# Transposes of P once per kv-head in half-height pairs, with Q/K loads apart from V loads, in a grouped-query attention kernel

## Chip, cores, metric

One core of one Trainium2 chip. The metric is the device time of one execution in microseconds (us), median of several runs.

## The reference

```python
B, Hq, Hkv, Sq, Sk, D = 8, 16, 8, 256, 512, 256      # q, k, v in bf16
k = jnp.repeat(k, 2, axis=1)                          # two query heads share one kv-head
v = jnp.repeat(v, 2, axis=1)
scores = jnp.einsum("bhqd,bhkd->bhqk", q, k) * D ** -0.5
p = softmax(scores, axis=-1)
return jnp.einsum("bhqk,bhkd->bhqd", p, v)
```

There are 64 pairs of batch and kv-head ("heads" below). Each has 2 × 256 query rows, so four tiles of 128 rows ("steps"): 256 steps in all.

## The kernel before

Per step, TensorE makes scores S (2 matmuls, 512 columns), transposes the 128x512 tile of P (4 transposes of 128x128) and multiplies by V (4 matmuls, 257 columns; the 257th gives the row sums). VectorE finds the row minimum of the negated scores and copies the transposed P out of PSUM; ScalarE takes the exponential and copies the output out; GpSimd normalises. The tensor queue is software-pipelined: transposes run 2 steps and P·V 4 steps behind the scores.

```python
    LAG_PT = 2; LAG_PV = 4; LAG_OC = 4; LAG_RC = 5
    NSB = 3; NPTB = 2; NOB = 3; NP = 3; NPT = 4; NO = 20      # buffers
    # ... PSUM: S 3 banks, PT 2 banks, O 3 banks
        @block.vector
            for t in range(NSTEP + LAG_RC):
                # ... minimum of step t (L217), then
                u = t - LAG_PT
                    dve.wait_ge(sem_PT, u + 1)
                    dve.tensor_copy(                                   # L227
                        PT_sb[:, u % NPT, :, :],
                        PT_ps[:, u % NPTB, 0:NC * P].rearrange("p (c q) -> p c q", c=NC),
                    ).then_inc(sem_PTe, 1)
        @block.tensor
            for t in range(NSTEP + LAG_PV):
                # ... scores of step t, two matmuls (L268)
                w = t - LAG_PT
                if 0 <= w < NSTEP:
                    pe.wait_ge(sem_P, w + 1)
                    if w >= NPTB:
                        pe.wait_ge(sem_PTe, w - NPTB + 1)
                    for c in range(NC):
                        mm = pe.transpose(                             # L281
                            PT_ps[:, w % NPTB, c * P:(c + 1) * P],
                            P_sb[:, w % NP, c * P:(c + 1) * P],
                            ident[:],
                        )
                    mm.then_inc(sem_PT, 1)
                # ... P.V of step t - LAG_PV, four matmuls (L300)
        @block.sync
            for pi, (b, h0, h1) in enumerate(pieces):
                # ... waits; load Q and K of the piece with DMA transposes, then its V
```

## Time and profile before

| | before |
|---|---|
| time | 293.57 us (293.41 to 293.71, 13 runs) |
| span of the profile | 291.7 us |
| PE / DVE / ACT busy | 98% / 93% / 85% |
| one head (4 steps), from scores to the next head's scores | 4.38 us |

"Busy" counts an engine as busy while any record of it is open. TensorE's records overlap (a transpose's is 219 ns long, and the next one starts 56 ns after it), so its costs are read from the distances between starts. The prediction shows the lines and how they are read.

### The profile page before, as it was taken

Reading aid. Unit: us, or ns where it says so; the run is one execution under the profiler, and the core shown is the slowest. Engines: PE = TensorE matmul, PEld = TensorE weight load, DVE = VectorE, ACT = ScalarE, POOL = GpSimd, SP = SyncE. Lnnn points to the kernel's source line nnn. Section 1 sums busy time; section 2 is a strip of 40 time slices with the busy share of each in tenths; the row PEclk is TensorE's granted clock in tenths of the full one; section 3 lists DMA queues with packets and bytes.
Section 4 is the critical chain, followed back from the end, with each engine's and each line's share of the span. In section 5 each row is a group of like instructions: output and inputs, shape, how many; then the busy total and the mean of one; then the engine's idle time right before and its main releaser. Section 6 shows DMA issues by size and latency. Waiting matters only on the chain.

```text
span 291.7 us, 8061 instructions
## 1 busy us (share of the span) xinstructions
PE 284.9 (98%) x2570; PEld 215.3 (74%) x2570; DVE 270.9 (93%) x839; ACT 248.3 (85%) x514; POOL 116.9 (40%) x259
## 2 busy tenths in 40 slices
PE   7999999999999999999999999999999999999994
PEld 2677777777777777777777777777777777777772
DVE  1999999999999999999999999999999999999995
ACT  2888888888888888888888888888888888888883
POOL 1053353353353353353453453453453453453452
PEclk9999999999999999999999999999999999999999
DMA  6999999999999999999999999999999999941103
GB/s 157 231 212 247 186 264 226 256 219 253 210 337 234 183 277 221 357 236 218 253 347 243 218 234 272 327 236 219 245 359 213 215 225 276 399 174 72 74 36 112
DMA packets 154953, 67.64 MB, mean 232 GB/s; under 512 B 133792, under 2 KB 140192, under 8 KB 154912
## 3 DMA queue, kind: packets, MB, share of 16 engines
q1 hardware_dynamic: 154912, 67.12, 100.2%
q8 instruction: 22, 0.36, 0.5%
q14 instruction: 19, 0.16, 0.2%
HBM read 16.78 MB, written 16.78 MB: 115 GB/s over the span
## 4 chain that ended last, share of the span: by engine, by line
PE 95%; DMA 1%; DVE 1%; ACT 0%; SPq 0%; issue 0%; ACTq 0%
PE O_ps L300 38%; PE S_ps L268 38%; PE PT_ps L281 20%; DMA KT<-in_k_dram 1%; DVE out_sb L241 1%; ACT P_sb L207 0%; SPq L138 0%; DVE junk L217 0%; DVE rc L239 0%; DVE PT_sb L227 0%; ACT O_sb L193 0%; ACTq L192 0%
## 5 line engine op out<-in xcount | busy, mean ns | idle before, releaser
L217 DVE TENSOR_SCALAR_CACHE_REDUCE junk<-S_ps 128x512 bf16<-128x512 f32 x256 | 177.0, 692 | 17.3 <-PE S_ps L268 6.2
L182 POOL TENSOR_SCALAR out_sb<-O_sb,rc 128x256 bf16<-128x256 f32 x252 | 116.0, 479 | 170.4 <-DVE rc L247 170.4
L207 ACT ACTIVATE P_sb<-S_ps,bias 128x512 bf16<-128x512 f32 x256 | 177.4, 693 | 5.0 <-DVE junk L217 5.0
L300 PE MATMUL O_ps<-Vn,PT_sb 128*128 128x257 bf16 x1024 | 154.1, 273 | 0.0
L268 PE MATMUL S_ps<-KT,QT 128*128 128x512 bf16 x512 | 151.9, 379 | 1.2 <-DMA KT<-in_k_dram 1.0
L193 ACT COPY O_sb<-O_ps 128x257 f32<-128x257 f32 x256 | 95.5, 373 | 34.1 <-PE O_ps L300 1.0
L281 PEld LDWEIGHTS PT_ps<-ident,P_sb 128*128 128x128 bf16 x1024 | 78.3, 98 | 57.9 <-ACT P_sb L207 2.2
L227 DVE COPY PT_sb<-PT_ps 128x512 bf16<-128x512 bf16 x256 | 107.4, 420 | 0.6 <-PE PT_ps L281 0.6
L281 PE MATMUL PT_ps<-ident,P_sb 128*128 128x128 bf16 x1024 | 99.0, 219 | 0.9 <-ACT P_sb L207 0.9
L300 PEld LDWEIGHTS O_ps<-Vn,PT_sb 128*128 128x128 bf16 x1024 | 89.6, 98 | 6.3
L268 PEld LDWEIGHTS S_ps<-KT,QT 128*128 128x128 bf16 x512 | 56.9, 113 | 5.3 <-issue 1.8
L217 DVE DVE_READ_ACCUMULATOR junk<-S_ps 128x1 f32 x256 | 21.3, 83 | 0.0
L247 DVE RECIPROCAL rc<-O_sb 128x4 f32<-128x4 f32 x63 | 10.6, 168 | 0.0
L253 PE MATMUL O_ps<-const-bfloat16-1.0 128*128 128x512 bf16 x10 | 3.8, 548 | 0.8 <-PEq L320 0.8
L253 PEld LDWEIGHTS O_ps<-const-bfloat16-1.0 128*128 128x128 bf16 x10 | 1.2, 132 | 2.8 <-issue 2.7
L198 ACT ACT_TABLE_LOAD x1 | 1.3, 1283 | 0.8 <-PEq L320 0.8
L241 DVE TENSOR_SCALAR out_sb<-O_sb,rc 128x256 bf16<-128x256 f32 x4 | 1.6, 400 | 0.1
L239 DVE RECIPROCAL rc<-O_sb 128x1 f32<-128x1 f32 x4 | 0.6, 149 | 0.0
L170 POOL MEMSET Vn<- 128x64 bf16 x1 | 0.4, 380 | 0.0
L166 POOL TENSOR_SCALAR_AFFINE_SELECT ident<-const-bfloat16-1.0 128x128 bf16<-128x128 bf16 x1 | 0.3, 292 | 0.0
L320 POOL MEMSET const-float32-0.0<- 128x1 f32 x1 | 0.1, 98 | 0.3 <-issue 0.3
L165 POOL MEMSET warm<- 128x2 f32 x1 | 0.1, 99 | 0.3 <-POOLq L320 0.3
(4 smaller groups left out, 0.5 us busy)
## 6 DMA issues: line engine op xcount, KB each, us to landing
out_dram<-out_sb SPq DMA_DIRECT2D x63, 256.0 KB, 4.5
Vn<-in_v_dram SPq DMA_DIRECT2D x4, 512.0 KB, 4.5
Vn<-in_v_dram SPq DMA_DIRECT2D x4, 256.0 KB, 3.2
QT<-in_q_dram SPq DMA_TRANSPOSE x21, 9.4
KT<-in_k_dram SPq DMA_TRANSPOSE x21, 6.3
Vn<-in_v_dram SPq DMA_DIRECT2D x13, 0.5 KB, 6.2
out_dram<-out_sb SPq DMA_DIRECT2D x1, 192.0 KB, 2.5
out_dram<-out_sb SPq DMA_DIRECT2D x1, 64.0 KB, 2.2
```

Of the source, the lines that this page charges most:

```text
L182: last = g.tensor_scalar(out_sb[:, o_sl, j, :], O_sb[:, os_sl, j, 0:D], rc_t[:, os_sl, j:j + 1], 1.0, op0=ALU.mult, op1=ALU.mult,)
L193: act.copy(O_sb[:, it % NOS, j, :], O_ps[:, u % NOB, 0:D + 1]).then_inc(sem_Oc, 1)
L198: act.activation(warm[:, 1:2], warm[:, 0:1], ACTF.Exp)
L207: act.activation(P_sb[:, t % NP, :], S_ps[:, t % NSB, 0:Sk], ACTF.Exp, bias=bias_t[:, t % NBS:t % NBS + 1], scale=scale,).then_inc(sem_P, 1)
L217: dve.tensor_scalar(junk[:, t % 4, :], S_ps[:, t % NSB, 0:Sk], -scale, None, op0=ALU.mult, op1=ALU.min, accum_out=bias_t[:, t % NBS:t % NB ...
L227: dve.tensor_copy(PT_sb[:, u % NPT, :, :], PT_ps[:, u % NPTB, 0:NC * P].rearrange("p (c q) -> p c q", c=NC),).then_inc(sem_PTe, 1)
L241: dve.tensor_scalar(out_sb[:, it % NO, j, :], O_sb[:, it % NOS, j, 0:D], rc_t[:, it % NOS, j:j + 1], None, op0=ALU.mult,).then_inc(sem_nor ...
L247: dve.reciprocal(rc_t[:, it % NOS, :], O_sb[:, it % NOS, :, D]).then_inc(sem_rc, 1)
L253: pe.matmul(O_ps[:, NOB - 1, 0:512], lhsT=c_one[:, 0:P], rhs=c_one, start=True, stop=True)
L268: mm = pe.matmul(S_ps[:, t % NSB, 0:Sk], lhsT=QT[:, sl, dc, hh * RQ + j:(hh + 1) * RQ:NT], rhs=KT[:, sl, dc, hh * Sk:(hh + 1) * Sk], start ...
L281: mm = pe.transpose(PT_ps[:, w % NPTB, c * P:(c + 1) * P], P_sb[:, w % NP, c * P:(c + 1) * P], ident[:],)
L300: mm = pe.matmul(O_ps[:, u % NOB, 0:D + 1], lhsT=PT_sb[:, u % NPT, c, :], rhs=Vn[:, (sl * Hkv + hh) * NC + c, 0:D + 1], start=(c == 0), st ...
```

## The change

The intent: a transpose of a 128x128 block is split into the two blocks of 64 rows of P. Each is a matmul on its own half of the array's rows with N = 64, and two on different halves should run together. The whole head is done in one batch, so the array changes its tiling twice per head and not twice per step. P·V follows three heads later, the copies become two of 128x1024 per head, V gets its own order of loading, Q/K a third buffer, and the output buffers go from 20 to 16.

```diff
-    LAG_PT = 2
-    LAG_PV = 4
+    LAGC_PV = 3
+    PTB_POS = NT - 2 if NT >= 2 else 0
+    NQK = 3
-    NP = 3
+    NP = 2 * NT
-    NO = 20
+    NO = 2 * Hkv
 # ... Q/K pieces 1,1,1,1,2,2 / 2,2,4 / 4,4 heads; V pieces 1,1,2,2,2 / 2,2,4 / 4,4
+    for i, (b, h0, h1) in enumerate(v_pieces):
+        ev.append((b * Hkv + h0 + LAGC_PV - 0.25, 1, "v", i))
 # ... VectorE, after the third and the fourth minimum of a head:
+                dve.tensor_copy(
+                    PT_sb[:, i % NPTS, :, 64 * h:64 * h + 64],
+                    PT_ps[:, h, 0:NT * NC * 64].rearrange("p (m q) -> p m q", q=64),
+                ).then_inc(sem_PTe, 1)
 # ... TensorE:
+            def issue_PTB(i):
+                pe.wait_ge(sem_P, (i + 1) * NT)
+                if i >= 1:
+                    pe.wait_ge(sem_PTe, 2 * i)
+                for j in range(NT):
+                    slot = (i * NT + j) % NP
+                    for cc in range(NC):
+                        m = j * NC + cc
+                        for h in range(2):
+                            mm = pe.transpose(
+                                PT_ps[:, h, m * 64:(m + 1) * 64],
+                                P_sb[64 * h:64 * h + 64, slot, cc * P:(cc + 1) * P],
+                                ident[64 * h:64 * h + 64, 64 * h:64 * h + 64],
+                                tile_position=(64 * h, 0),
+                            )
+                mm.then_inc(sem_PT, 1)
+            for c in range(NIT + LAGC_PV):
+                for j in range(NT):
+                    # scores (c, j); P.V (c - LAGC_PV, j); at j == PTB_POS the batch of c - 1
```

More of the change, by code (lines that the diff above doesn't have):

```diff
@@ L30, in bass_standalone__gqa_softmax__near_ridge_kernel @@
     assert Sk <= 512 and D + 1 <= 512
+    assert NT * NC * 64 <= 1024
     NIT = B * Hkv
@@ L33, in bass_standalone__gqa_softmax__near_ridge_kernel @@
     scale = float(D) ** -0.5
-    LAG_PT = 2
-    LAG_PV = 4
-    LAG_OC = 4
-    LAG_RC = 5
+    LAGC_PV = 3
+    PTB_POS = NT - 2 if NT >= 2 else 0
+    LAG_OC = LAGC_PV * NT
+    NQK = 3
+    NVS = 2
     NSB = 3
-    NPTB = 2
     NOB = 3
-    NP = 3
-    NPT = 4
+    NP = 2 * NT
+    NPTS = 3
     NBS = 8
+    NJ = 4
     NOS = 3
-    NO = 20
+    NO = 2 * Hkv
     NWARM = 10
@@ L60, in split_plan @@
         return res
-    pieces = []
+    qk_pieces = []
+    v_pieces = []
+    sp_order = []
     for b in range(B):
         if b == 0:
-            plan = split_plan([1, 1, 1, 1, 2, 2])
+            qk_plan = split_plan([1, 1, 1, 1, 2, 2])
+            v_plan = split_plan([1, 1, 2, 2, 2])
         elif b == 1:
-            plan = split_plan([2, 2, 4])
-        else:
-            plan = split_plan([4, 4])
-        for (h0, h1) in plan:
-            pieces.append((b, h0, h1))
-    piece_of_it = {}
-    for pi, (b, h0, h1) in enumerate(pieces):
-        for hh in range(h0, h1):
-            piece_of_it[b * Hkv + hh] = pi
+            qk_plan = split_plan([2, 2, 4])
+            v_plan = split_plan([2, 2, 4])
+        else:
+            qk_plan = split_plan([4, 4])
+            v_plan = split_plan([4, 4])
+        qk_idx = []
+        for (h0, h1) in qk_plan:
+            qk_idx.append(len(qk_pieces))
+            qk_pieces.append((b, h0, h1))
+        v_idx = []
+        for (h0, h1) in v_plan:
+            v_idx.append(len(v_pieces))
+            v_pieces.append((b, h0, h1))
+    ev = []
+    for i, (b, h0, h1) in enumerate(qk_pieces):
+        ev.append((b * Hkv + h0, 0, "qk", i))
+    for i, (b, h0, h1) in enumerate(v_pieces):
+        ev.append((b * Hkv + h0 + LAGC_PV - 0.25, 1, "v", i))
+    ev.sort()
+    sp_order = [(kind, i) for (_, _, kind, i) in ev]
+    qk_piece_of_it = {}
+    for pi, (b, h0, h1) in enumerate(qk_pieces):
+        for hh in range(h0, h1):
+            qk_piece_of_it[b * Hkv + hh] = pi
+    v_piece_of_it = {}
+    for pi, (b, h0, h1) in enumerate(v_pieces):
+        for hh in range(h0, h1):
+            v_piece_of_it[b * Hkv + hh] = pi
     q_b = [q[b].rearrange("h s d -> (h s) d") for b in range(B)]
@@ L82, in bass_standalone__gqa_softmax__near_ridge_kernel @@
         block = ctx.enter_context(nc.Block())
-        QT = ctx.enter_context(nc.sbuf_tensor("QT", [P, 2, ND, RB], BF16))
-        KT = ctx.enter_context(nc.sbuf_tensor("KT", [P, 2, ND, KB], BF16))
-        Vn = ctx.enter_context(nc.sbuf_tensor("Vn", [P, 2 * Hkv * NC, VW], BF16))
+        QT = ctx.enter_context(nc.sbuf_tensor("QT", [P, NQK, ND, RB], BF16))
+        KT = ctx.enter_context(nc.sbuf_tensor("KT", [P, NQK, ND, KB], BF16))
+        Vn = ctx.enter_context(nc.sbuf_tensor("Vn", [P, NVS * Hkv * NC, VW], BF16))
         P_sb = ctx.enter_context(nc.sbuf_tensor("P_sb", [P, NP, Sk], BF16))
-        PT_sb = ctx.enter_context(nc.sbuf_tensor("PT_sb", [P, NPT, NC, P], BF16))
-        junk = ctx.enter_context(nc.sbuf_tensor("junk", [P, 4, Sk], BF16))
+        PT_sb = ctx.enter_context(nc.sbuf_tensor("PT_sb", [P, NPTS, NT * NC, P], BF16))
+        junk = ctx.enter_context(nc.sbuf_tensor("junk", [P, NJ, Sk], BF16))
         bias_t = ctx.enter_context(nc.sbuf_tensor("bias", [P, NBS], F32))
@@ L93, in bass_standalone__gqa_softmax__near_ridge_kernel @@
         ident = ctx.enter_context(nc.sbuf_tensor("ident", [P, P], BF16))
-        ones_t = ctx.enter_context(nc.sbuf_tensor("ones_t", [P, P], BF16))
         warm = ctx.enter_context(nc.sbuf_tensor("warm", [P, 2], F32))
         S_ps = ctx.enter_context(nc.psum_tensor("S_ps", [P, NSB, 512], F32))
-        PT_ps = ctx.enter_context(nc.psum_tensor("PT_ps", [P, NPTB, 1024], BF16))
+        PT_ps = ctx.enter_context(nc.psum_tensor("PT_ps", [P, 2, 1024], BF16))
         O_ps = ctx.enter_context(nc.psum_tensor("O_ps", [P, NOB, 512], F32))
-        sem_qt = [ctx.enter_context(nc.semaphore(f"sem_qt{i}")) for i in range(len(pieces))]
-        sem_kt = [ctx.enter_context(nc.semaphore(f"sem_kt{i}")) for i in range(len(pieces))]
-        sem_v = [ctx.enter_context(nc.semaphore(f"sem_v{i}")) for i in range(len(pieces))]
+        sem_qt = [ctx.enter_context(nc.semaphore(f"sem_qt{i}")) for i in range(len(qk_pieces))]
+        sem_kt = [ctx.enter_context(nc.semaphore(f"sem_kt{i}")) for i in range(len(qk_pieces))]
+        sem_v = [ctx.enter_context(nc.semaphore(f"sem_v{i}")) for i in range(len(v_pieces))]
         sem_setup = ctx.enter_context(nc.semaphore("sem_setup"))
@@ L113, in bass_standalone__gqa_softmax__near_ridge_kernel @@
         sem_stb = [ctx.enter_context(nc.semaphore(f"sem_stb{i}")) for i in range(NSTB)]
-        sem_g = ctx.enter_context(nc.semaphore("sem_g"))
         sem_stl = ctx.enter_context(nc.semaphore("sem_stl"))
@@ L118, in bass_standalone__gqa_softmax__near_ridge_kernel @@
         assert NO >= 2 * Hkv
+        last_split = NT >= 2
         @block.sync
@@ L124, in stores_of_batch @@
                     dst = o_b[b2][hh2 * RQ:(hh2 + 1) * RQ, :].rearrange("(p j) d -> p j d", j=NT)
-                    if it2 < NIT - 1 or NT < 2:
+                    if it2 < NIT - 1 or not last_split:
                         sp.wait_ge(sem_norm, it2 + 1)
@@ L132, in stores_of_batch @@
                         sp.dma_start(dst[:, NT - 1:NT, :], out_sb[:, it2 % NO, NT - 1:NT, :]).then_inc(sem_stl, 16)
-            for pi, (b, h0, h1) in enumerate(pieces):
-                sl = b % 2
-                if b >= 2 and h0 == 0:
-                    sp.wait_ge(sem_S, (b - 1) * Hkv * NT)
-                sp.dma_start_transpose(
-                    QT[:, sl, :, h0 * RQ:h1 * RQ], q_b[b][h0 * RQ:h1 * RQ, :]
-                ).then_inc(sem_qt[pi], 16)
-                sp.dma_start_transpose(
-                    KT[:, sl, :, h0 * Sk:h1 * Sk], k_b[b][h0 * Sk:h1 * Sk, :]
-                ).then_inc(sem_kt[pi], 16)
-                if b >= 2 and h0 == 0:
-                    sp.wait_ge(sem_PV, (b - 1) * Hkv * NT)
-                vb = (sl * Hkv + h0) * NC
-                ve = (sl * Hkv + h1) * NC
-                sp.dma_start(
-                    Vn[:, vb:ve, 0:D],
-                    v[b, h0:h1].rearrange("h (c p) d -> p (h c) d", c=NC),
-                ).then_inc(sem_v[pi], 16)
-                if b >= 2 and h1 == Hkv:
+            nload_left = {}
@@ new lines, in _ @@
+            for (kind, pi) in sp_order:
+                bb = (qk_pieces if kind == "qk" else v_pieces)[pi][0]
+                nload_left[bb] = nload_left.get(bb, 0) + 1
+            for (kind, pi) in sp_order:
+                if kind == "qk":
+                    b, h0, h1 = qk_pieces[pi]
+                    sl = b % NQK
+                    if b >= NQK and h0 == 0:
+                        sp.wait_ge(sem_S, (b - NQK + 1) * Hkv * NT)
+                    sp.dma_start_transpose(
+                        QT[:, sl, :, h0 * RQ:h1 * RQ], q_b[b][h0 * RQ:h1 * RQ, :]
+                    ).then_inc(sem_qt[pi], 16)
+                    sp.dma_start_transpose(
+                        KT[:, sl, :, h0 * Sk:h1 * Sk], k_b[b][h0 * Sk:h1 * Sk, :]
+                    ).then_inc(sem_kt[pi], 16)
+                else:
+                    b, h0, h1 = v_pieces[pi]
+                    if b >= NVS and h0 == 0:
+                        sp.wait_ge(sem_PV, (b - NVS + 1) * Hkv * NT)
+                    vsl = b % NVS
+                    vb = (vsl * Hkv + h0) * NC
+                    ve = (vsl * Hkv + h1) * NC
+                    sp.dma_start(
+                        Vn[:, vb:ve, 0:D],
+                        v[b, h0:h1].rearrange("h (c p) d -> p (h c) d", c=NC),
+                    ).then_inc(sem_v[pi], 16)
+                nload_left[b] -= 1
+                if b >= 2 and nload_left[b] == 0:
@@ L159, in _ @@
                     sp.wait_ge(sem_stb[i], 16 * Hkv * n_i)
-            if NT >= 2:
+            if last_split:
                 sp.wait_ge(sem_stl, 16)
@@ L173, in _ @@
                 o_sl = it % NO
-                if it == NIT - 1 and NT >= 2:
+                if it == NIT - 1 and last_split:
                     break
@@ L205, in _ @@
                     if t >= NP:
-                        act.wait_ge(sem_PT, t - NP + 1)
+                        act.wait_ge(sem_PT, (t - NP) // NT + 1)
                     act.activation(
@@ L213, in _, with evac, recip_norm @@
         def _(dve):
-            for t in range(NSTEP + LAG_RC):
+            def evac(i, h):
+                dve.wait_ge(sem_PT, i + 1)
+                if h == 0 and i >= NPTS:
+                    dve.wait_ge(sem_PV, (i - NPTS + 1) * NT)
+                dve.tensor_copy(
+                    PT_sb[:, i % NPTS, :, 64 * h:64 * h + 64],
+                    PT_ps[:, h, 0:NT * NC * 64].rearrange("p (m q) -> p m q", q=64),
+                ).then_inc(sem_PTe, 1)
+            def recip_norm(w):
+                it, j = divmod(w, NT)
+                if it == NIT - 1 and last_split:
+                    dve.wait_ge(sem_Oc, w + 1)
+                    if j == 0 and it >= NO:
+                        bb = (it - NO) // Hkv
+                        dve.wait_ge(sem_stb[bb % NSTB], 16 * Hkv * (bb // NSTB + 1))
+                    dve.reciprocal(rc_t[:, it % NOS, j:j + 1], O_sb[:, it % NOS, j, D:D + 1]).then_inc(sem_rcl, 1)
+                    dve.wait_ge(sem_rcl, j + 1)
+                    dve.tensor_scalar(
+                        out_sb[:, it % NO, j, :], O_sb[:, it % NOS, j, 0:D],
+                        rc_t[:, it % NOS, j:j + 1], None, op0=ALU.mult,
+                    ).then_inc(sem_norml, 1)
+                elif j == NT - 1:
+                    dve.wait_ge(sem_Oc, (it + 1) * NT)
+                    dve.reciprocal(rc_t[:, it % NOS, :], O_sb[:, it % NOS, :, D]).then_inc(sem_rc, 1)
+            LAG_RC = LAG_OC + 1
+            for t in range(NSTEP + LAG_RC + NT):
                 if t < NSTEP:
@@ L217, in _ @@
                     dve.tensor_scalar(
-                        junk[:, t % 4, :], S_ps[:, t % NSB, 0:Sk], -scale, None,
+                        junk[:, t % NJ, :], S_ps[:, t % NSB, 0:Sk], -scale, None,
                         op0=ALU.mult, op1=ALU.min,
@@ L221, in _ @@
                     ).then_inc(sem_bias, 1)
-                u = t - LAG_PT
-                if 0 <= u < NSTEP:
-                    dve.wait_ge(sem_PT, u + 1)
-                    if u >= NPT:
-                        dve.wait_ge(sem_PV, u - NPT + 1)
-                    dve.tensor_copy(
-                        PT_sb[:, u % NPT, :, :],
-                        PT_ps[:, u % NPTB, 0:NC * P].rearrange("p (c q) -> p c q", c=NC),
-                    ).then_inc(sem_PTe, 1)
+                c, j = divmod(t, NT)
+                if 0 <= c - 1 < NIT:
+                    if j == NT - 2 or NT == 1:
+                        evac(c - 1, 0)
+                    if j == NT - 1:
+                        evac(c - 1, 1)
                 w = t - LAG_RC
                 if 0 <= w < NSTEP:
-                    it, j = divmod(w, NT)
-                    if it == NIT - 1 and NT >= 2:
-                        dve.wait_ge(sem_Oc, w + 1)
-                        if j == 0 and it >= NO:
-                            bb = (it - NO) // Hkv
-                            dve.wait_ge(sem_stb[bb % NSTB], 16 * Hkv * (bb // NSTB + 1))
-                        dve.reciprocal(rc_t[:, it % NOS, j:j + 1], O_sb[:, it % NOS, j, D:D + 1]).then_inc(sem_rcl, 1)
-                        dve.wait_ge(sem_rcl, j + 1)
-                        dve.tensor_scalar(
-                            out_sb[:, it % NO, j, :], O_sb[:, it % NOS, j, 0:D],
-                            rc_t[:, it % NOS, j:j + 1], None, op0=ALU.mult,
-                        ).then_inc(sem_norml, 1)
-                    elif j == NT - 1:
-                        dve.wait_ge(sem_Oc, (it + 1) * NT)
-                        dve.reciprocal(rc_t[:, it % NOS, :], O_sb[:, it % NOS, :, D]).then_inc(sem_rc, 1)
+                    recip_norm(w)
         @block.tensor
@@ L254, in _ @@
             pe.wait_ge(sem_setup, 2)
-            for t in range(NSTEP + LAG_PV):
-                if t < NSTEP:
-                    it, j = divmod(t, NT)
-                    b, hh = divmod(it, Hkv)
-                    sl = b % 2
-                    if j == 0:
-                        pi = piece_of_it[it]
-                        if it == pieces[pi][0] * Hkv + pieces[pi][1]:
-                            pe.wait_ge(sem_qt[pi], 16)
-                            pe.wait_ge(sem_kt[pi], 16)
-                    if t >= NSB:
-                        pe.wait_ge(sem_P, t - NSB + 1)
-                    for dc in range(ND):
-                        mm = pe.matmul(
-                            S_ps[:, t % NSB, 0:Sk],
-                            lhsT=QT[:, sl, dc, hh * RQ + j:(hh + 1) * RQ:NT],
-                            rhs=KT[:, sl, dc, hh * Sk:(hh + 1) * Sk],
-                            start=(dc == 0), stop=(dc == ND - 1),
-                        )
-                    mm.then_inc(sem_S, 1)
-                w = t - LAG_PT
-                if 0 <= w < NSTEP:
-                    pe.wait_ge(sem_P, w + 1)
-                    if w >= NPTB:
-                        pe.wait_ge(sem_PTe, w - NPTB + 1)
-                    for c in range(NC):
-                        mm = pe.transpose(
-                            PT_ps[:, w % NPTB, c * P:(c + 1) * P],
-                            P_sb[:, w % NP, c * P:(c + 1) * P],
-                            ident[:],
-                        )
-                    mm.then_inc(sem_PT, 1)
-                u = t - LAG_PV
-                if 0 <= u < NSTEP:
-                    it, j = divmod(u, NT)
-                    b, hh = divmod(it, Hkv)
-                    sl = b % 2
-                    pe.wait_ge(sem_PTe, u + 1)
-                    if j == 0:
-                        pi = piece_of_it[it]
-                        if it == pieces[pi][0] * Hkv + pieces[pi][1]:
-                            pe.wait_ge(sem_v[pi], 16)
-                    if u >= NOB:
-                        pe.wait_ge(sem_Oc, u - NOB + 1)
-                    for c in range(NC):
-                        mm = pe.matmul(
-                            O_ps[:, u % NOB, 0:D + 1],
-                            lhsT=PT_sb[:, u % NPT, c, :],
-                            rhs=Vn[:, (sl * Hkv + hh) * NC + c, 0:D + 1],
-                            start=(c == 0), stop=(c == NC - 1),
-                        )
-                    mm.then_inc(sem_PV, 1)
@@ new lines, in issue_S @@
+            def issue_S(ts):
+                it, j = divmod(ts, NT)
+                b, hh = divmod(it, Hkv)
+                sl = b % NQK
+                if j == 0:
+                    pi = qk_piece_of_it[it]
+                    if it == qk_pieces[pi][0] * Hkv + qk_pieces[pi][1]:
+                        pe.wait_ge(sem_qt[pi], 16)
+                        pe.wait_ge(sem_kt[pi], 16)
+                if ts >= NSB:
+                    pe.wait_ge(sem_P, ts - NSB + 1)
+                for dc in range(ND):
+                    mm = pe.matmul(
+                        S_ps[:, ts % NSB, 0:Sk],
+                        lhsT=QT[:, sl, dc, hh * RQ + j:(hh + 1) * RQ:NT],
+                        rhs=KT[:, sl, dc, hh * Sk:(hh + 1) * Sk],
+                        start=(dc == 0), stop=(dc == ND - 1),
+                    )
+                mm.then_inc(sem_S, 1)
@@ new lines, in issue_PTB @@
+            def issue_PTB(i):
+                pe.wait_ge(sem_P, (i + 1) * NT)
+                if i >= 1:
+                    pe.wait_ge(sem_PTe, 2 * i)
+                mm = None
+                for j in range(NT):
[8 more added lines that the diff above has]
+                                tile_position=(64 * h, 0),
+                            )
+                mm.then_inc(sem_PT, 1)
@@ new lines, in issue_PV @@
+            def issue_PV(u):
+                it, j = divmod(u, NT)
+                b, hh = divmod(it, Hkv)
+                vsl = b % NVS
+                if j == 0:
+                    pe.wait_ge(sem_PTe, 2 * (it + 1))
+                    pi = v_piece_of_it[it]
+                    if it == v_pieces[pi][0] * Hkv + v_pieces[pi][1]:
+                        pe.wait_ge(sem_v[pi], 16)
+                if u >= NOB:
+                    pe.wait_ge(sem_Oc, u - NOB + 1)
+                for cc in range(NC):
+                    mm = pe.matmul(
+                        O_ps[:, u % NOB, 0:D + 1],
+                        lhsT=PT_sb[:, it % NPTS, j * NC + cc, :],
+                        rhs=Vn[:, (vsl * Hkv + hh) * NC + cc, 0:D + 1],
+                        start=(cc == 0), stop=(cc == NC - 1),
+                    )
+                mm.then_inc(sem_PV, 1)
@@ L310 @@
+            for c in range(NIT + LAGC_PV):
+                for j in range(NT):
+                    if c < NIT:
+                        issue_S(c * NT + j)
+                    if 0 <= c - LAGC_PV < NIT:
+                        issue_PV((c - LAGC_PV) * NT + j)
+                    if j == PTB_POS and 0 <= c - 1 < NIT:
+                        issue_PTB(c - 1)
 _INS = ['q', 'k', 'v']
```

## The prediction

> **What bounds the kernel now.** I read the busy shares first, then the chain that ended last, then the costliest groups, then one step of the steady state in the timeline. The first two:
>
> ```profile
> PE 284.9 (98%) x2570; PEld 215.3 (74%) x2570; DVE 270.9 (93%) x839; ACT 248.3 (85%) x514; POOL 116.9 (40%) x259
> ...
> PE 95%; DMA 1%; DVE 1%; ACT 0%; SPq 0%; issue 0%; ACTq 0%
> PE O_ps L300 38%; PE S_ps L268 38%; PE PT_ps L281 20%; DMA KT<-in_k_dram 1%; DVE out_sb L241 1%; ACT P_sb L207 0%; SPq L138 0%; DVE junk L217 0%; DVE rc L239 0%; DVE PT_sb L227 0%; ACT O_sb L193 0%; ACTq L192 0%
> ```
>
> TensorE (PE) is the chain: scores (L268) 38%, P transposes (L281) 20%, P·V (L300) 38%. No DMA is in it after the first K load. The groups say what each piece of work costs; the last number before the second bar is the mean ns of one instruction:
>
> ```profile
> L217 DVE TENSOR_SCALAR_CACHE_REDUCE junk<-S_ps 128x512 bf16<-128x512 f32 x256 | 177.0, 692 | 17.3 <-PE S_ps L268 6.2
> L207 ACT ACTIVATE P_sb<-S_ps,bias 128x512 bf16<-128x512 f32 x256 | 177.4, 693 | 5.0 <-DVE junk L217 5.0
> L281 PEld LDWEIGHTS PT_ps<-ident,P_sb 128*128 128x128 bf16 x1024 | 78.3, 98 | 57.9 <-ACT P_sb L207 2.2
> L227 DVE COPY PT_sb<-PT_ps 128x512 bf16<-128x512 bf16 x256 | 107.4, 420 | 0.6 <-PE PT_ps L281 0.6
> L281 PE MATMUL PT_ps<-ident,P_sb 128*128 128x128 bf16 x1024 | 99.0, 219 | 0.9 <-ACT P_sb L207 0.9
> ```
>
> The matmul durations overlap, so they are no cost; distances between starts are. One steady step of the timeline (first column the start in us, second the length):
>
> ```profile
> 150.20 0.59 PE L268 MATMUL S_ps<-KT,QT 128*128 128x512 bf16 x2
> 150.36 0.08 DVE L217 DVE_READ_ACCUMULATOR junk<-S_ps 128x1 f32 x1
> 150.36 0.42 DVE L227 COPY PT_sb<-PT_ps 128x512 bf16<-128x512 bf16 x1
> ...
> 150.63 0.39 PE L281 MATMUL PT_ps<-ident,P_sb 128*128 128x128 bf16 x4
> ...
> 150.84 0.69 DVE L217 TENSOR_SCALAR_CACHE_REDUCE junk<-S_ps 128x512 bf16<-128x512 f32 x1
> 150.86 0.60 PE L300 MATMUL O_ps<-Vn,PT_sb 128*128 128x257 bf16 x4
> ...
> 151.30 0.59 PE L268 MATMUL S_ps<-KT,QT 128*128 128x512 bf16 x2
> ```
>
> Differences of starts: two score matmuls 0.43 us, four transposes 0.23 us (56 to 57 ns each), four P·V matmuls 0.44 us, together 1.10 us with no gap. A kv-head is four steps, 4.38 us: 1.74 us of scores, 0.90 us of transposes, 1.75 us of P·V. 64 heads make 280 us of the 291.7 us span; the rest is 5.5 us until the first K has landed and about 7 us after the last scores. The gain or loss is therefore 64 times the change of what PE, or whichever engine takes its place, needs for one head.
>
> VectorE (DVE) is close behind. From the timeline's start, where nothing holds it, the minimum (L217) repeats every 0.61 to 0.62 us:
>
> ```profile
> 6.16 0.69 DVE L217 TENSOR_SCALAR_CACHE_REDUCE junk<-S_ps 128x512 bf16<-128x512 f32 x1 [6.16 <-PE S_ps L268]
> ...
> 6.78 0.69 DVE L217 TENSOR_SCALAR_CACHE_REDUCE junk<-S_ps 128x512 bf16<-128x512 f32 x1
> ...
> 7.39 0.69 DVE L217 TENSOR_SCALAR_CACHE_REDUCE junk<-S_ps 128x512 bf16<-128x512 f32 x1
> ```
>
> Per head: 4 × 0.617 + 4 × 0.42 + 0.15 (reciprocal, mostly hidden part left out) = 4.30 us of 4.38. In the steady step the copy ends at 150.78 and the minimum starts at 150.84, just after the scores it needs: DVE waits for PE by some 0.06 us a step. ACT needs about 0.61 + 0.27 us a step, 3.5 us a head.
>
> [...] The kernel before uses one mode only (128*128 in every row)[...]. [...] The trace shows 98 ns for 128 columns, mostly hidden behind the matmul before; no run here shows yet how closely loads can follow each other. [...]
>
> **The change part by part.**
>
> *DVE copies.* 256 copies of 128x512 (420 ns) become 128 of 128x1024. [...] Per head 2 × 0.69 = 1.37 us in place of 1.68. DVE per head: 4 × 0.617 + 1.37 + 0.15 = 3.99 us. That becomes the floor of the whole kernel.
>
> *Transposes.* The 16 of a head (N = 128, whole array) become 32 of half height with N = 64, in pairs on rows 0-63 and 64-127, each with its own load, issued in one batch per head. Old cost 0.90 us. [...]
>
> *Mode switches.* Two per head, before and after the batch[...]. My estimate, from the 98 ns load, is 0.05 to 0.15 us each, 0.1 to 0.3 us a head.
>
> *Lag.* P·V of a head runs three heads after its scores instead of four steps. The PE work is the same, but at the end 12 P·V steps (12 × 0.44) and one batch remain after the last scores, and the reverse gap at the start is filled at DVE's pace. The last scores of before begin at 283.79, and 7.5 us follow their end; I count 10.5 us now. The start: 5.5 us, then some 2.7 us for the first head (four minima at 0.62). So span = 5.5 + 2.7 + 63 × p + 10.5, with p the period of one head, and the time is 1.9 us above the span, as before (293.58 against 291.7).
>
> *V and Q/K loads apart, a third Q/K buffer.* PE waits for no load in the steady state (1.0 us for K in all), so I count nothing.
>
> *Sum.* PE per head is 1.74 + 1.75 = 3.49 us plus batch and switches. Working case: 0.50 + 0.15 = 0.65, so p = 4.14 us; DVE at 3.99 is just under it. Time = 18.7 + 63 × 4.14 + 1.9 = 281.4 us. I predict 281 us.
>
> **The rivals.**
>
> *Loads or issue set the pace, not the columns streamed.* [...] For it: a whole-array load takes 98 ns in the rows and each half-transpose has one of the same width, so load work doubles. Against it: that 98 is a latency; loads have so far always started behind a matmul and never been late. [...]
>
> *DVE becomes the bound.* If pairs overlap fully and the switch is cheap (0.10), PE needs 4.09 at most and DVE's 3.99 is in reach: 18.7 + 63 × 3.99 + 1.9 = 272 us. For it: DVE was at 93%. Against: any time DVE waits for the end of the batch is lost to it.
>
> *A new wait.* There is one set of transpose banks: a batch waits until both copies of the head before are done, and the first copy waits for the whole batch. The first copy is placed after the third minimum of the head; that minimum ends about 0.78 us after its scores, the batch about 0.44 + 0.65 = 1.09. So DVE idles up to 0.3 us there if it is not behind anyway, and 3.99 + 0.3 = 4.29 would then be p: 291 us, within 2%. Against: DVE has slack elsewhere only if PE is the bound, and three score banks let it catch up.
>
> *DMA.* The queue is at work through five sixths of the span, but PE waits for none of it; a period of 4.1 us takes away 6% of the slack. I give this little.
>
> **Range and chances.** p = 3.99 (DVE floor) gives 272; faster by 2% (under 287.7 us) needs p under 4.24, so a batch with its switches under 0.75 us; slower by 2% (over 299.5) needs p above 4.43, a batch over 0.94. Pairs that overlap, with cheap switches, are likely but nothing in the trace of before shows them, and the loads are the open point: faster 0.58, same 0.15, slower 0.27. Range 269 to 308 us: it runs from a little under the DVE floor to the case of loads that set the pace with cheap switches.
>
> **What would show it right or wrong.** Right: starts of pairs of transposes about 30 ns apart; the batch with its gaps under 0.7 us; the copy of 128x1024 near 0.69 us; DVE over 95% busy; the share of the transposes in the chain down from 20% to about 14%. Wrong: [...]gaps above 0.15 us at both ends of a batch, or DVE idle before the copies with PE as releaser. If the time is above 300 us, the step that failed is the overlap of the pairs or their loads; if it is below 270, the DVE floor.

## The result

The changed kernel takes 284.55 us (284.31 to 285.16, 8 runs; a ninth execution, 285.34, is not in the median) against 293.57: ratio 0.9696, 95% interval 0.9686 to 0.9705, so 3.0% faster. All ratios here are the mean time of one kernel's runs over that of the other's in the same rounds, so not quite the ratio of the quoted medians. Executions over 1.5% slower than the fastest of the same kernel are left out of the means.

The page of the changed kernel, its busy line, the chain that ended last, and the groups that answer to those shown of before:

```profile
PE 273.1 (96%) x3594; PEld 186.6 (66%) x3594; DVE 249.7 (88%) x711; ACT 238.2 (84%) x514; POOL 116.7 (41%) x259
...
PE S_ps L312 41%; PE O_ps L350 39%; PE PT_ps L330 13%; DMA KT<-in_k_dram 1%; DVE junk L278 1%; ACT P_sb L241 1%; DVE out_sb L266 1%; SPq L168 0%; DVE PT_sb L252 0%; DVE rc L264 0%; ACT O_sb L227 0%
...
L252 DVE COPY PT_sb<-PT_ps 128x1024 bf16<-128x1024 bf16 x128 | 88.1, 689 | 20.0 <-PE PT_ps L330 19.7
...
L330 PEld LDWEIGHTS PT_ps<-ident,P_sb 64*128 64x128 bf16 x2048 | 33.4, 95 | 14.0 <-ACT P_sb L241 12.7
L330 PE MATMUL PT_ps<-ident,P_sb 64*128 64x64 bf16 x2048 | 41.0, 191 | 0.0
```

PE still sets the end. The transposes have doubled in number, but their share of the chain fell from 20% to 13%. "64*128" is the tiling as the trace gives it: each is alone on half of the rows. Every other matmul keeps 128*128.

The timeline of the changed kernel around one batch (start in us, length):

```profile
151.66 0.69 ACT L241 ACTIVATE P_sb<-S_ps,bias 128x512 bf16<-128x512 f32 x1
...
153.29 0.60 PE L350 MATMUL O_ps<-Vn,PT_sb 128*128 128x257 bf16 x4
...
153.82 0.52 PEld L330 LDWEIGHTS PT_ps<-ident,P_sb 64*128 64x128 bf16 x32 [0.21 <-ACT P_sb L241]
153.83 0.64 PE L330 MATMUL PT_ps<-ident,P_sb 64*128 64x64 bf16 x32
...
154.40 0.62 PE L312 MATMUL S_ps<-KT,QT 128*128 128x512 bf16 x2
154.51 0.69 DVE L252 COPY PT_sb<-PT_ps 128x1024 bf16<-128x1024 bf16 x1 [0.32 <-PE PT_ps L330]
...
155.12 0.68 DVE L278 TENSOR_SCALAR_CACHE_REDUCE junk<-S_ps 128x512 bf16<-128x512 f32 x1
...
158.58 0.41 PE L312 MATMUL S_ps<-KT,QT 128*128 128x512 bf16 x1
```

32 transposes in 0.64 us, the last of which is 0.19 long: (0.64 - 0.19) / 31 = 14.5 ns from start to start on average. The single records of the trace show what that is: the two of a pair start 3 to 4 ns apart, and the next pair 29 ns after the last. So a pair of half-transposes takes 29 ns where a whole transpose took 56. From P·V's first start (153.29) to the batch is 0.54 us, where four P·V matmuls need 0.44; the batch to the scores takes 0.57 where 16 × 29 ns is 0.46; the scores take 0.03 us more. These 0.22 us (206 - 110 ns ahead, 123 - 27 ns behind and 30 ns in the scores, by the single records) are what a visit to the other tiling costs; 110 ns is the distance of the P·V matmuls, and 25 to 27 ns that from the second of a pair to the next pair. The single records show the loads late at both places: the batch's first load starts 202 ns after the start of the last P·V matmul, and the scores' first load 118 ns after that of the last transpose, where most loads (3074 of 3582 from 20 us on) start 1 or 2 ns after the matmul ahead. The profile puts the 0.21 us before the batch down to ScalarE's P, but the last exponential that this batch needs is the one shown at 151.66; it ended 1.5 us before. From scores to scores one head later it is 158.58 - 154.40 = 4.18 us instead of 4.38.

Where the 8.6 us of the two spans went, by the starts of the heads' first scores:

| part of the span | before | after |
|---|---|---|
| to the first scores | 5.5 | 5.8 |
| heads 0 to 3 | 16.6 | 15.6 |
| 59 heads in the steady state | 258.4 | 246.9 |
| head 63 to the end | 11.2 | 14.8 |

The steady state gives 11.5 us. The longer lag gives 3.6 us back at the end, as P·V of three heads is left there. In exchange the first three heads run without P·V, so the first four heads take 1 us less, though they have a wait that the kernel before has not. In the timeline of the changed kernel, first the issue of the fifth and sixth heads' K, then PE:

```profile
15.16 3.97 SPq L171 DMA_TRANSPOSE KT<-in_k_dram  x1
...
21.39 0.60 PE L312 MATMUL S_ps<-KT,QT 128*128 128x512 bf16 x2 [1.72 <-issue]
```

The table of DMA issues gives 6.1 us from this issue to landing, so 21.26; the scores start 0.13 us later. The profile calls the wait "issue", but it is the wait for this K. In the kernel before, the same K was issued at 16.54 and landed 5.2 us later, at 21.7; the fifth head's scores began there at 22.09, so it came just in time.

The waits of the changed kernel (total us, times, longest):

```profile
DVE PT_sb L252 <- PE PT_ps L330: 19.7, 60, 0.9
POOL out_sb L216 <- DMA out_dram<-out_sb: 19.4, 5, 5.4
```

Both are new: VectorE stands 0.32 us before the first copy of nearly every head, and GpSimd waits for stores; the later runs with 20 output buffers have no such wait. Whether either costs time is a question for the experiments.

### The profile page after: what moved, and what is told of

It is laid out like the page before. It is cut to its first block, busy times and chain, and to the rows that moved or that the text cites. A ratio compares the mean times of both kernels' runs of the same rounds, so it can differ in the third digit from the quotient of the medians.

```text
span 283.1 us, 9407 instructions
## 1 busy us (share of the span) xinstructions
PE 273.1 (96%) x3594; PEld 186.6 (66%) x3594; DVE 249.7 (88%) x711; ACT 238.2 (84%) x514; POOL 116.7 (41%) x259
## 4 chain that ended last, share of the span: by engine, by line
PE 93%; DVE 2%; DMA 1%; issue 1%; ACT 1%; SPq 0%
PE S_ps L312 41%; PE O_ps L350 39%; PE PT_ps L330 13%; DMA KT<-in_k_dram 1%; DVE junk L278 1%; ACT P_sb L241 1%; DVE out_sb L266 1%; SPq L168 0%; DVE PT_sb L252 0%; DVE rc L264 0%; ACT O_sb L227 0%
## 5 line engine op out<-in xcount | busy, mean ns | idle before, releaser
L278 DVE TENSOR_SCALAR_CACHE_REDUCE junk<-S_ps 128x512 bf16<-128x512 f32 x256 | 172.9, 679 | 8.5 <-PE S_ps L312 8.4
L312 PE MATMUL S_ps<-KT,QT 128*128 128x512 bf16 x512 | 153.7, 383 | 4.6 <-issue 1.7
L350 PEld LDWEIGHTS O_ps<-Vn,PT_sb 128*128 128x128 bf16 x1024 | 100.1, 98 | 60.2
L252 DVE COPY PT_sb<-PT_ps 128x1024 bf16<-128x1024 bf16 x128 | 88.1, 689 | 20.0 <-PE PT_ps L330 19.7
L312 PEld LDWEIGHTS S_ps<-KT,QT 128*128 128x128 bf16 x512 | 51.8, 116 | 14.7 <-issue 4.7
L330 PEld LDWEIGHTS PT_ps<-ident,P_sb 64*128 64x128 bf16 x2048 | 33.4, 95 | 14.0 <-ACT P_sb L241 12.7
L330 PE MATMUL PT_ps<-ident,P_sb 64*128 64x64 bf16 x2048 | 41.0, 191 | 0.0
```

What stands on the lines that cost most here:

```text
L252: dve.tensor_copy(PT_sb[:, i % NPTS, :, 64 * h:64 * h + 64], PT_ps[:, h, 0:NT * NC * 64].rearrange("p (m q) -> p m q", q=64),).then_inc(se ...
L278: dve.tensor_scalar(junk[:, t % NJ, :], S_ps[:, t % NSB, 0:Sk], -scale, None, op0=ALU.mult, op1=ALU.min, accum_out=bias_t[:, t % NBS:t % N ...
L312: mm = pe.matmul(S_ps[:, ts % NSB, 0:Sk], lhsT=QT[:, sl, dc, hh * RQ + j:(hh + 1) * RQ:NT], rhs=KT[:, sl, dc, hh * Sk:(hh + 1) * Sk], star ...
L330: mm = pe.transpose(PT_ps[:, h, m * 64:(m + 1) * 64], P_sb[64 * h:64 * h + 64, slot, cc * P:(cc + 1) * P], ident[64 * h:64 * h + 64, 64 * ...
L350: mm = pe.matmul(O_ps[:, u % NOB, 0:D + 1], lhsT=PT_sb[:, it % NPTS, j * NC + cc, :], rhs=Vn[:, (vsl * Hkv + hh) * NC + cc, 0:D + 1], star ...
```

## The experiments

The theory: PE sets the pace throughout, the gain is the pairs of half-transposes that run together, and the price is the change of tiling. Rivals: the gain is from bigger copies or from the loads; the gaps around a batch are waits for data; VectorE's wait for the batch is on the path.

### Whole transposes again, all else as changed

```diff
-                        for h in range(2):
-                            mm = pe.transpose(PT_ps[:, h, m * 64:(m + 1) * 64], P_sb[64 * h:64 * h + 64, ...], ..., tile_position=(64 * h, 0))
+                        mm = pe.transpose(PT_ps[:, m // 8, (m % 8) * P:(m % 8 + 1) * P], P_sb[:, slot, cc * P:(cc + 1) * P], ident[:])
```
(The copies are adapted; their size stays 128x1024.)

> The changed kernel with whole-array transposes again (16 of N = 128 per head, one batch, no change of tiling mode); copies, lag and loads stay as changed. Theory (the gain is the overlap of half-height pairs): starts 56 ns apart, batch 0.90 us, no gap at its ends (110 ns from the last P.V start before it, 56 ns to the scores after it), head period 3.49 + 0.90 = 4.38 us instead of 4.18, so about 284.6 + 60 x 0.20 = 296 us, slower than the kernel before by about 1%. Rival (the gain is the bigger copies, the batching or the loads): period stays near 4.18, 284 to 287 us.

296.04 us (295.89 to 297.66), ratio 1.0084. PE's timeline in this run:

```profile
152.28 0.59 PE L312 MATMUL S_ps<-KT,QT 128*128 128x512 bf16 x2
...
155.33 0.60 PE L348 MATMUL O_ps<-Vn,PT_sb 128*128 128x257 bf16 x4
155.77 1.06 PE L329 MATMUL PT_ps<-ident,P_sb 128*128 128x128 bf16 x16
156.66 0.59 PE L312 MATMUL S_ps<-KT,QT 128*128 128x512 bf16 x2
```

The batch follows P·V after 0.44 us, with no gap; it takes 0.89 us to the next scores; the period is 156.66 - 152.28 = 4.38 us, as before the change. So batching, bigger copies and the new loads together win nothing in the steady state; the half-height pairs carry all of it. Without them the change is 0.8% slower, mostly by the longer end (from the last minimum to the end of the span 11.1 us, against 7.3 before the change). This run also waits for the fifth head's K:

```profile
21.75 0.59 PE L312 MATMUL S_ps<-KT,QT 128*128 128x512 bf16 x2 [1.65 <-issue]
```

Its heads are as long as before the change, so shorter heads are not what makes that K late. The first heads without P·V are: the fourth head's first minimum is at 17.0 us here and at 18.3 in the kernel before, and this K lands at 21.65, no sooner than there.

### Two batches per head

```diff
-                    if j == PTB_POS and 0 <= c - 1 < NIT:
-                        issue_PTB(c - 1)
+                    if j in (PTB_POS - 1, PTB_POS) and 0 <= c - 1 < NIT:
+                        issue_PTB(c - 1, j - PTB_POS + 1)      # steps 0,1 and steps 2,3
```
(`issue_PTB` makes the half of a head that its second argument names; only the second half signals VectorE.)

> The same 32 half-transposes per head, but in two batches of 16, one after the second and one after the third P.V group; copies unchanged, so twice as many mode changes and nothing else. Theory (each visit to the 64-row mode costs about 0.22 us: 206 - 110 ns ahead, 123 - 27 ns behind, 30 ns in the scores after it): period 4.18 + 0.22 = 4.40 us, about 298 us. Rival (the gaps around the batch are waits for P or for the copies of the head before, which are there once per head): 285 to 288 us.

298.91 us (298.01 to 299.21), ratio 1.0177. PE's timeline, one head:

```profile
154.46 0.60 PE L351 MATMUL O_ps<-Vn,PT_sb 128*128 128x257 bf16 x4
154.99 0.41 PE L330 MATMUL PT_ps<-ident,P_sb 64*128 64x64 bf16 x16
...
155.79 0.60 PE L351 MATMUL O_ps<-Vn,PT_sb 128*128 128x257 bf16 x4
156.33 0.41 PE L330 MATMUL PT_ps<-ident,P_sb 64*128 64x64 bf16 x16
156.67 0.62 PE L312 MATMUL S_ps<-KT,QT 128*128 128x512 bf16 x2
```

Both batches have the same 0.53 to 0.54 us from P·V's first start, and the period, taken between the heads' first minima on VectorE (median over all heads), is 4.41 us against 4.18. The second visit costs 0.23 us. The second batch needs nothing that the first did not have, and whole transposes behind the same waits had no gap. So the gaps belong to the change of tiling, not to P or to the copies. That is why the change batches: two visits per head already eat the gain, and the kernel is then slower than before.

### Same instructions, neighbours on the same half

```diff
-                for j in range(NT):
-                    ...
-                        for h in range(2):
+                for h in range(2):
+                    for j in range(NT):
+                        ...
```

> The same instructions per head, only in another order: all 16 of rows 0-63 first, then all 16 of rows 64-127, so neighbours share a row group. Theory (the two of a pair run together, 29 ns a pair): [...]batch about 0.85 us in place of 0.48, period about 4.57, 308 us or a little more[...]. Rival (a half-transpose is simply cheap, order does not matter): 285 us.

306.98 us (306.65 to 307.37), ratio 1.0457. PE's timeline:

```profile
151.41 1.00 PE L330 MATMUL PT_ps<-ident,P_sb 64*128 64x64 bf16 x32
...
155.96 1.00 PE L330 MATMUL PT_ps<-ident,P_sb 64*128 64x64 bf16 x32
```

(1.00 - 0.19) / 31 = 26 ns is only the mean of the distances. By the single records, neighbours on one half start 29 to 30 ns apart (1472 of the 1984 distances inside batches). Where the order passes from one half to the other, the starts read as two interleaved series of 29 ns each: the last four of rows 0-63 run together with the first four of rows 64-127, although the queue lists them one after the other. From batch to batch it is 4.55 us. Only the order differs, and it is worth 22 us: a half-transpose by itself costs half a whole one (29 ns of 56), and the pair wins because its second is free (29 ns for both). The weight loads, one per half-transpose and 95 ns long on average, keep up with 29 ns even on one half of the rows, and with 29 ns per pair on two. So a load's length is not its pace (in the kernel before, loads 98 ns long start 56 ns apart), and loads that come one by one at their own length are ruled out. One thing stays open: each half writes its own PSUM bank (`PT_ps[:, h]`), so in this order neighbours share the bank as well as the rows, and no run separates the two.

### Loads coupled again, two Q/K buffers

```diff
-    NQK = 3
+    NQK = 2
-            v_plan = split_plan([1, 1, 2, 2, 2])
+            v_plan = split_plan([1, 1, 1, 1, 2, 2])
-        ev.append((b * Hkv + h0 + LAGC_PV - 0.25, 1, "v", i))
+        ev.append((b * Hkv + h0, 1, "v", i))
```

> V loads again directly behind the Q and K of the same piece, and two Q/K buffers instead of three; all else as changed. Theory (loads count only at the start): steady period still 4.18 us; the wait for Q/K of the fifth head at the start (1.7 us in the changed kernel) grows by one V load, 0.6 us or somewhat more; 284.5 to 287 us. Rival (the separate loads or the third buffer carry part of the gain in the steady state): period above 4.25 and over 289 us.

285.79 us (285.24 to 287.9), ratio 0.9748 (0.9710 to 0.9787). The steady period is 4.18 us as before this edit. What differs lies in the first five heads: in the profiled execution, the slowest of the four, the sixth head's first minimum comes at 29.4 us instead of 26.6. Beside the changed kernel's 0.9696 the loads' part of the change (order and third buffer together) is worth about 0.5%, 1.2 us by the medians and so more than the 0.6 expected; the interval nearly reaches down to the changed kernel's.

### Four small copies per head

```diff
-                dve.tensor_copy(PT_sb[:, i % NPTS, :, 64 * h:64 * h + 64], PT_ps[:, h, 0:1024]...)
+                for s in range(2):
+                    dve.tensor_copy(PT_sb[:, i % NPTS, 8 * s:8 * s + 8, 64 * h:64 * h + 64], PT_ps[:, h, 512 * s:512 * s + 512]...)
```
(The semaphore counts follow: four copies per head in place of two.)

> The four copies of 128x512 per head again (two per bank, one behind the other); transposes as changed. DVE work per head grows by 4 x 0.42 - 2 x 0.69 = 0.30 us, from about 3.86 to 4.16 of a 4.18 us period. Theory (PE is the bound, and DVE's 0.32 us wait for the batch is only its slack): the wait shrinks by about 0.3 us, the period stays within 4.18 to 4.25, 284.5 to 289 us. Rival (DVE with its wait for the batch is the bound, so the copies' size is what was won): period 4.18 + 0.30 = 4.48, about 302 us.

285.45 us (284.8 to 285.56), ratio 0.9713; the period is 4.18 us. VectorE's timeline in this run:

```profile
153.86 0.76 DVE L253 COPY PT_sb<-PT_ps 128x512 bf16<-128x512 bf16 x2 [0.26 <-PE PT_ps L331]
154.53 0.68 DVE L279 TENSOR_SCALAR_CACHE_REDUCE junk<-S_ps 128x512 bf16<-128x512 f32 x1
```

VectorE's wait shrank from 0.32 to 0.26 and the period did not move, so this wait is slack. But it shrank by 0.06 us, not by the expected 0.3: two copies of 0.42 us take 0.76 together, and the next instruction starts 0.67 us after the first of them. In the changed kernel one copy of 0.69 us lets the next start after 0.61 (154.51 to 155.12 in its timeline). VectorE's lengths overlap as PE's do. So this run loads VectorE with only 2 × (0.67 - 0.61) = 0.12 us a head more, not 0.30. The test is weaker than planned, but it holds: with VectorE as the bound the period would be 4.18 + 0.12 = 4.30 by this estimate.

### Where the start and the end could be shortened

Six runs tried to take back what the start and the end cost. Differences of some 0.3% between them mean little: with the same loads, PE's wait that the profile calls "issue" was 1.7 us in the changed kernel and 0.7 us in the run with small copies. First smaller pieces, for the 1.7 us wait (`qk_plan = split_plan([1, 1, 1, 1, 1, 1, 2])` for the first batch):

> Q and K of the first batch in pieces of 1,1,1,1,1,1,2 heads instead of 1,1,1,1,2,2. Theory (the changed kernel loses 1.7 to 1.9 us at 19.5 us because the fifth head's K comes in a piece of two heads and lands at about 21.3 us): the wait goes, 282.7 us. Rival (the wait is for something else, a V load or a bank): 284.5 us.

285.48 us (285.0 to 285.83), ratio 0.9717: nothing won. The wait moved to the next piece of two heads (heads 8 and 9), and was longer:

```profile
38.70 0.60 PE L312 MATMUL S_ps<-KT,QT 128*128 128x512 bf16 x2 [2.14 <-issue]
```

That piece's K was issued at 32.04 and landed 6.6 us later, at 38.64. Second, the batch and its copies one P·V group earlier (`PTB_POS = NT - 3`, copies after the second and third minimum):

> The batch and its two copies one P.V group earlier in the head. Theory (PE is the bound; where in the head the batch stands is indifferent as long as P and banks are there): period 4.18 us, 284 to 285.5 us. Rival (the place of the batch was needed: P or the banks are late): new gaps before the batch, period above 4.25, over 289 us.

285.71 us (284.88 to 286.48), ratio 0.9720, period 4.18 us. The place is indifferent to the period, as the theory has it; the profiled run lost 1.7 us at one later head, which makes its time a little worse than expected. Third, on top of both, P·V two heads behind (`LAGC_PV = 2`):

> The early batch, P.V two heads behind the scores instead of three, and the small first pieces. Theory (at the end one head's P.V less remains, 4 x 0.44 us, and the start's wait of 1.9 us is gone): 284.55 - 1.75 - 1.9 = 281 us, if the second copy of a head is done before its P.V starts. Rival (P.V then waits for the second copy each head): period above 4.18, 284 us or more.

286.27 us, the median of six. One of them was slow (289.6); the five fast ones spread over 284.12 to 287.58, ratio 0.9729 (0.9697 to 0.9760). The period is 4.18 us and the end did shrink by 1.7 us (from the last minimum to the last engine's end), yet a wait near head 21 ate it. The timeline of this run follows it through three engines:

```profile
95.12 7.32 POOL L216 TENSOR_SCALAR out_sb<-O_sb,rc 128x256 bf16<-128x256 f32 x16 [11.67 <-DMA out_dram<-out_sb]
97.06 0.38 ACT L227 COPY O_sb<-O_ps 128x257 f32<-128x257 f32 x1 [2.98 <-POOL out_sb L216]
...
98.07 0.62 PE L312 MATMUL S_ps<-KT,QT 128*128 128x512 bf16 x2 [2.09 <-ACT P_sb L241]
```

GpSimd waits 11.7 us for a store to free an output buffer, ScalarE then for GpSimd, and PE for ScalarE. This is the new store wait of the changed kernel; there it is at most 5.4 us and ScalarE never waits for GpSimd, here it comes through. So the next runs went back to 20 output buffers. With single-head Q/K pieces through the first batch and 1,1,1,1,2,2 in the second:

> Q and K in pieces of one head through the first batch and of 1,1,1,1,2,2 in the second, and 20 output buffers as in the kernel before; all else as changed. Theory (the start is short of load rate, so a piece of two heads too early makes PE wait for its second head; with six small pieces the wait only moved to the first two-head piece): the wait at the start shrinks from about 1.9 us to under 0.5, 282.5 to 283.5 us. Rival (the loads are behind in total, whatever their pieces): a wait of the same 1.9 us further on, 284.5 us or more.

287.06 us (286.34 to 288.5), ratio 0.9778 (0.9756 to 0.9801): worse than the changed kernel. The wait is now 2.65 us at the third batch, at its first piece of four heads:

```profile
72.48 0.59 PE L312 MATMUL S_ps<-KT,QT 128*128 128x512 bf16 x2 [2.65 <-issue]
```

Its K was issued at 64.62 and took 7.8 us: 72.42. The rival held: in the first 70 us the loads keep only just ahead of PE, and the wait falls where the next big piece stands. Up to that wait SyncE's queue shows its load instructions end to end, with no gap over 0.5 us. Whether issuing them or moving the data sets this rate, no run separates. GpSimd's wait for stores is gone from the waits of this run. With the two-head lag as well:

> The same with the early batch and P.V two heads behind. Theory (the end is shorter by 1.7 us, as in the run with small pieces, whose gain was eaten by waits for output buffers and loads): 281 to 282 us. Rival (waits for stores come back although there are 20 output buffers): 283 us or more.

285.12 us (284.51 to 287.29), ratio 0.9720: missed too, by the same wait at the third batch. Last, 20 buffers, early batch and the two-head lag, with the pieces of the changed kernel:

> Early batch, P.V two heads behind and 20 output buffers, but the pieces of the changed kernel. Theory: the wait at the start stays, the end is shorter by 1.7 us: 282.5 to 284 us. Rival (16 output buffers were not what held the run with lag two at its heads 21 and 22): waits of some us in mid-run, 285 us or more.

284.38 us (284.03 to 284.55), ratio 0.9679 (0.9667 to 0.9692). The waits in mid-run are gone (with the buffers the pieces changed back too, so the trace of the run that waited for stores, not this comparison, is what names the stores), and this is the best, but its interval overlaps that of the changed kernel (0.9686 to 0.9705), so it is not shown to be better.

## Why the prediction was right, and where it was off

The mechanism held: a pair of half-transposes took 29 ns. 281 us were predicted and 284.55 measured, inside 269 to 308; "faster" had been given 0.58. By the prediction's own sum the span would be 279.5 us, and it is 283.1: 0.8 us more up to the fifth head, 2.6 in the 59 heads after it (4.184 instead of 4.14 us each), 0.2 from the last head's first scores on (what follows its scores is 0.6 longer, its scores are done 0.4 sooner than a whole period).

- **PE stays the bound.** Right: 93% of the chain, 4.18 us a head against the predicted 4.14. S and P·V kept their 3.49 us.
- **The pairs overlap.** Right: 29 ns a pair, so 0.48 us a batch; the 0.50 in the prediction's sum was its author's estimate. Undoing it alone brings back 4.38 us; breaking only the order gives 4.55. The rival of loads that set the pace falls with the same two runs. Half-transposes on one half start 29 ns apart, and their loads, 95 ns long, keep that pace.
- **Tiling changes.** The term was mis-sized: 0.15 us a head in the sum, 0.22 in the trace and 0.23 in the run with two batches, still in the range given. Over 59 heads that is 4.1 us, from which the pairs, 0.02 us a head cheaper than estimated, take 1.2.
- **The end.** 10.5 us from the end of the last scores, measured 11.1 (they start at 271.82 and take 0.22, and the span is 283.1).
- **The start.** "I count nothing" for the loads was the step that failed in kind: the lag leaves the first three heads without P·V, they reach the fifth head's K before it has landed, and PE waits 1.7 us. The run with whole transposes shows that shorter heads are not needed for it, the runs with smaller pieces that the loads as a whole are behind.
- **VectorE.** The copy was 689 ns; the predicted 0.69 us was its author's estimate. From 420 ns for 512 elements to 689 for 1024 it is (689 - 420) / 512 = 0.525 ns per element. But the floor built from it, 3.99 us a head, was too high, and "DVE over 95% busy" was wrong (88%). I took the copies at their full length, though the next instruction starts before a copy's record ends (0.61 us after it began). The trace of before shows it too:

```profile
150.36 0.42 DVE L227 COPY PT_sb<-PT_ps 128x512 bf16<-128x512 bf16 x1
...
150.69 0.17 DVE L247 RECIPROCAL rc<-O_sb 128x4 f32<-128x4 f32 x1
```

The reciprocal starts 0.33 us after the copy, which is open for 0.42. So VectorE had more room before the change than the prediction's 0.06 us a step, and the range's lower end was no hard floor.

- **The new wait** of VectorE on the batch, up to 0.3 us, came at 0.32, and it stood among the signs of being wrong. But neither that sign nor the figure of 4.29 us for it held: the run with small copies shows the wait to be slack.
- **A sum.** The split of the old span (5.5, 280 and 7 us) adds up to 1 us more than the 291.7: the first four heads take 16.6 us and not 4 × 4.38.

## What to carry to other kernels

In this kernel TensorE was the bound, and its transposes were 20% of the chain. Two half-height transposes on different row halves (here in different PSUM banks too) took 29 ns where a whole one took 56, but only with the two side by side in the queue: with neighbours on the same half each took 29 ns, and the kernel 306.98 us. The batch also had to be long enough to pay for the change of tiling: here 0.23 us against 0.42 us won by 16 pairs, and with two visits a head the kernel took 298.91 us. Before counting on a saving in one stage, ask what it takes to feed it: first heads without P·V came before their loads (1.7 us of wait), and two attempts to move that wait with smaller pieces found the next big piece just as late (waits of 2.14 and 2.65 us). Fewer output buffers stopped one schedule here and, as far as the traces show, not the other: with 16, GpSimd's longest wait for a store was 5.4 us at the three-head lag, where ScalarE never waited for GpSimd, and 11.7 us at the two-head lag, where PE then stood for 2.09 us.
